# Two feed-forward layers behind a two-part attention: token blocks of 512 in three of four passes, x split chunk by chunk

## The chip, the cores and the metric

The kernel runs on one core of one Trainium2 chip. The metric is device time in microseconds of one execution; the time before is the median of three runs. A profiled execution has its own time, which stands beside its span below. TensorE (PE) has two granted clock levels, 1.2 and 2.4 GHz; the profile gives the granted clock as a share of full speed.

## The reference, cut to what matters

```python
# q, k, v: (4 batches, 8 heads, 576 positions, 64), float32
# per head: out = repeat(softmax_attention(mean4(q), mean4(k), mean4(v)), 4) + banded_attention(q, k, v, |i-j| < 4)
x = attn_out.transpose(0, 2, 1, 3).reshape(2304, 512)
h = x @ moe_w_in            # (2304, 512) @ (512, 2048)
x = silu(h) @ moe_w_out     # (2304, 2048) @ (2048, 512)
h = x @ moe2_w_in
out = elu(h) @ moe2_w_out   # (2304, 512)
```

## The kernel before

Activations lie transposed in SBUF as `x32`: 128 partitions (features within a chunk) by `KC` = 4 chunks of 128 features by 2304 tokens. Chunk c holds the heads of head pair c. A feed-forward product is made of three fp32r products (high times high, high times low, low times high), so each operand is split in a high part (`xh`, `wh`, `gh`) and a low part (`xl`, `wl`, `gl`); the high part is a cast on ACT, the low part a subtraction on DVE or POOL.

Each of the two layers runs in `NPASS` = 2 passes over the tokens, one for each half of the 16 blocks of 128 hidden features; a pass is written (layer, pass). Within a pass the loop runs over token blocks n (layer 0: nine blocks of 256; layer 1: six blocks of 384; `NBS`), and in a block over the `FP` = 8 hidden blocks f. One (layer, pass, n, f) is a unit; there are 72, 72, 48 and 48 of them. A unit has

- `g1` (line 465): 12 matmuls (4 chunks by 3 products) of the block's width into one PSUM bank `ph` (two banks in turn);
- the activation chain: in layer 0 Tanh on ACT (L476) and a DVE product (L478); in layer 1 min on DVE (L481), Exp on ACT (L482), a DVE max (L484); then the cast `gh` on ACT (L486) and the subtraction `gl` on POOL (L488);
- `g2`, emitted `LAG` = 3 units later: in layer 0 (L516) 4 output chunks by 3 matmuls of 256 columns, weights stationary, two chunks sharing a PSUM bank; in layer 1 (L518) for each 128 tokens 3 matmuls of 512 columns, `g` stationary and weights moving.

The first pass of a layer stores its sums to DRAM (`ypart`), the second loads them (`part`, one buffer) and adds: in layer 0 back into `x32`, in layer 1 into the output. After the attention is over, six PSUM banks serve the sums in turn (`ybanks`).

`split_x` makes `xh` and `xl` of the next block: one tile of 4 chunks each, two buffers, so a whole block ahead; its steps stand in the list `spread`, from which `tick` emits one step after each group of `g2` matmuls. The same list carries the decoding of weights (`decode_w`: a load into one of three `ws` buffers on SP, L154 and L156 on ACT, L165, L166 and L172 on DVE), at most 18 weight tiles ahead of their split (`split_w`, L182 and L184), which takes place in the last block of a pass.

The attention of 16 head pairs (4 batches by `NPAIR` = 4) is a generator with `STEPS` = 19 steps, several pairs under way at once. The four pairs of batch 0 run ahead of the first unit, together with the decoding of the first weights; the other twelve are fed between the matmuls of pass (0, 0) by `tick`. Pairs 0 to 3 borrow memory: their transposed rows lie in `x32` (L199), the rows of pairs 1 and 2 in the `xh` and `xl` buffers (L217), and the scores `ED` of the pooled attention go over those rows later. Later pairs have `qk` and `qkD` tiles, two buffers each. The pooled result of 144 positions is copied from PSUM to `up` (L407), and one DVE operation (L424) adds it, each position read four times, to the banded result into `x32`.

All loads are issued on SP, but for four at the very start on ACT's queue (L549). A load waits for the one that used its completion semaphore before it.

Of the kernel before, what the change touches and what calls it, by code (L numbers as in the profile page):

```python
# [22 lines left out]
def attention_moe_moe2_kernel(ctx, tc, q, k, v, wi1, wo1, wi2, wo2, out):  # L23
    nc = tc.nc
# [9 lines left out]
    NBS = (2 * P, 3 * P)  # L34
    NBM = max(NBS)
# [165 lines left out]
    def load_rows(i, which, engine=None):  # L201
        b, h0 = pairs[i][0], 2 * pairs[i][1]
        src = (q, k, v)[which]
        if which == 2:

            if i < NPAIR:
                heads = [wpool.tile([P, DM], F32R, tag=tag, name="rows2").bitcast(F32) for tag in ("wh0", "wl0")]
            else:
                t = nat.tile([P, 4 * FAC * D], F32, tag="natv", name="rows2", bufs=1)
                heads = [t[:, :DM], t[:, DM:]]  # L210
            for j, t in enumerate(heads):
                (engine or nc.sync).dma_start(t[:HS], src[b, h0 + j].rearrange("(p r) d -> p (r d)", r=2 * FAC))
# [12 lines left out]
        for j in range(2):  # L225
            (engine or nc.sync).dma_start(t[:TB, :, j * D:(j + 1) * D], src[b, h0 + j].rearrange("(c p) d -> p c d", p=TB))
        loaded[i, which] = t
# [42 lines left out]
    def attention(i):  # L270
        b, pr = pairs[i]

        if i < NPAIR:
            qk = borrow(i, "qk")
            qkD = borrow(i, "qkD")
        else:
            qk = att.tile([P, 2 * S], F32, tag="qk", name="qk")
            qkD = att.tile([P, 2 * SD], F32, tag="qkD", name="qkD")
# [3 lines left out]
        for parts in ([(0, c) for c in range(NTB - 1)], [(1, c) for c in range(NTB - 1)], [(0, NTB - 1), (1, NTB - 1)]):  # L282
            ps = bank("pst")
            for n, (which, c) in enumerate(parts):
                nc.tensor.transpose(ps[:, n * TB:(n + 1) * TB], rows[which][:TB, c, :], ident[:TB, :TB])
# [49 lines left out]

        ED = borrowed[i][:, :4 * SD] if i < NPAIR else ring("ED", 4 * SD)
        ED = ED.rearrange("p (j a s) -> p j a s", j=2, a=2)
        sm = att.tile([P, 4], F32, tag="sm", name="sm", bufs=4)

        rl2 = att.tile([P, NW, 2], F32, tag="rl2", name="rl2", bufs=4)  # L340
        nc.gpsimd.memset(rl2[:, :, 1:2], EPS)
        rl = att.tile([P, NW, 1], F32, tag="rl", name="rl", bufs=4)
# [9 lines left out]
        for j in range(2):  # L352
            ps = psd[j]
            nm = att.tile([P, 2], F32, tag="nm", name="nm", bufs=4)
            nc.vector.tensor_reduce(
                nm[:HS], ps[:HS, :2 * SD].rearrange("p (a s) -> p a s", a=2), axis=AX.X, op=ALU.max, negate=True
            )
            yield
            for a in range(2):
                nc.scalar.activation(  # L360
                    ED[:HS, j, a, :], ps[:HS, a * SD:(a + 1) * SD], AF.Exp, bias=nm[:HS, a:a + 1],
                    accum_out=sm[:HS, 2 * j + a:2 * j + a + 1],
                )
# [10 lines left out]
        ED3 = ED.rearrange("p j a s -> p (j a) s")  # L374
        nc.gpsimd.tensor_tensor(
            ED3[:HS], ED3[:HS], sm.rearrange("p (n o) -> p n o", o=1)[:HS].to_broadcast([HS, 4, SD]), ALU.mult
        )
# [13 lines left out]
        for j in range(2):  # L391
            ps = bank("psD")
            for a in range(2):
                for c in range(2):
                    o = c * SD + a * HS
                    nc.tensor.transpose(ps[:HS, o:o + HS], ED[:HS, j, a, :].rearrange("p (m c) -> p c m", c=2)[:, c, :], ident[:HS, :HS])
# [3 lines left out]
        up = att.tile([P, SD], F32, tag="up", name="up")  # L400
# [6 lines left out]
        nc.scalar.copy(up, ps[:, :SD])  # L407
        yield
        for t in range(2):
            ps = bank("pso")  # L410
            for w in range(t * NW // 2, (t + 1) * NW // 2):
# [15 lines left out]
                up[:, u0:u0 + HALF // FAC].rearrange("p (m o) -> p m o", o=1).to_broadcast([P, HALF // FAC, FAC]),  # L427
# [7 lines left out]
    def split_x(layer, ps, n):  # L435
        nb = NBS[layer]
        src = x32[:, :, n * nb:(n + 1) * nb]
        hi = xs.tile([P, KC, NBM], F32R, tag="xh", name="xh")[:, :, :nb]
        lo = xs.tile([P, KC, NBM], F32R, tag="xl", name="xl")[:, :, :nb]
        xsplit[layer, ps, n] = (hi, lo)  # L440
        for c in range(KC + 1):
            if c < KC:
                nc.scalar.copy(hi[:, c, :], src[:, c, :])
            if c > 0:
                nc.vector.tensor_tensor(lo[:, c - 1, :], src[:, c - 1, :], hi[:, c - 1, :].bitcast(F32), ALU.subtract)  # L445
            yield

# [3 lines left out]
        (layer, ps, n, f) for layer in range(2) for ps in range(NPASS) for n in range(NT // NBS[layer])  # L451
        for f in range(FP)
    ]
    g_t = {}

    def g1(u, tick):
        layer, ps, n, f = u
        nb = NBS[layer]
# [3 lines left out]
        products = [(c, a, b) for c in range(KC) for a, b in ((w[0], x[0]), (w[0], x[1]))]  # L462
        products += [(c, w[1], x[0]) for c in range(KC)]
        for k, (c, a, b) in enumerate(products):
            nc.tensor.matmul(ph[:, :nb], a[:, c, :], b[:, c, :], start=k == 0, stop=k == 3 * KC - 1)  # L465
            if k % 3 == 2:
                tick(False)
        yield
# [23 lines left out]
    def g2(u, tick):  # L492
        layer, ps, n, f = u
        nb = NBS[layer]
        g = g_t.pop(u)
        w = wt[layer, ps * FP + f, 1]
        nd = KC if layer == 0 else nb // P
        if f == 0:
            acc[0] = [ybank(f"y{d}") for d in range(KC // 2 if layer == 0 else nd)]
            if ps == 1:  # L500
                part = yp.tile([P, 4 * NBM], F32, tag="y", name="part")
                nc.sync.dma_start(part[:, :nb * KC], ypart[layer, n])
# [3 lines left out]
        if f == FP - 1 and ps == 0:  # L506
            o = yp.tile([P, 4 * NBM], F32, tag="y", name="yo")
        for d in range(nd):
            sl = slice(d * P, (d + 1) * P)
            for m in range(3):  # L510
                wm, gm = w[m // 2], g[m % 2]
                first, last = (f == 0 and m == 0), (f == FP - 1 and m == 2)
                if layer == 0:

                    h = (d % 2) * nb
                    nc.tensor.matmul(y[d // 2][:, h:h + nb], wm[:, sl], gm, start=first and d % 2 == 0, stop=last, skip_group_check=True)  # L516
                else:
                    nc.tensor.matmul(y[d], gm[:, sl], wm, start=first, stop=last)  # L518
            if f < FP - 1:
                tick(True)  # L520
                continue
            if layer == 0 and d % 2 == 0:
                continue
            i, width = (d // 2, 2 * nb) if layer == 0 else (d, DM)
            part = slice(i * width, (i + 1) * width)
            if ps == 0:
                if i % 2 == 0:
                    nc.vector.tensor_scalar_mul(o[:, part], y[i][:, :width], sc)  # L528
                else:
                    nc.scalar.activation(o[:, part], y[i][:, :width], AF.Copy, scale=sc)  # L530
            elif layer == 0:
                nc.vector.scalar_tensor_tensor(
                    x32[:, d - 1:d + 1, n * nb:(n + 1) * nb],
                    y[i][:, :width].rearrange("p (a t) -> p a t", a=2), sc,
                    acc[1][:, part].rearrange("p (a t) -> p a t", a=2), op0=ALU.mult, op1=ALU.add,
                )
            else:
                src = acc[1][:, part]
                nc.vector.scalar_tensor_tensor(src, y[i], sc, src, op0=ALU.mult, op1=ALU.add)  # L539
                t0 = n * nb + d * P  # L540
                nc.sync.dma_start(out[t0:t0 + P, :], src)
        if f == FP - 1 and ps == 0:
            ypart[layer, n] = dram.tile([P, nb * KC], F32, tag=f"yp{layer}_{n}", name=f"yp{layer}_{n}")
            nc.sync.dma_start(ypart[layer, n], o[:, :nb * KC])

    with tc.manual_schedule():
# [24 lines left out]
        def small():  # L571
            while spread:
                try:
# [3 lines left out]
                    spread.pop(0)  # L577

# [142 lines left out]
        starts = [next(n_ for n_ in range(NT // NBS[0]) if (n_ + 1) * NBS[0] > b_ * S) for b_ in range(1, B)]  # L721
        deadline = [0] + [TICKS * (FP * (n_ - 1) + 6) for n_ in starts]

        for i in range(len(units) + LAG):
            if i < len(units):
                layer, ps, n, f = units[i]
                last = NT // NBS[layer] - 1
# [11 lines left out]
                need_first(2 * f + (3 if i < FP else 0))  # L739
                at["unit"] = i  # L740
# [4 lines left out]
                if n == last and (layer, ps) != (1, 1):  # L745
# [3 lines left out]
                if f >= (6 if attending else 2):  # L749
                    nx = (layer, ps, n + 1) if n < last else ((layer, 1, 0) if ps == 0 else (layer + 1, 0, 0))  # L750
                    if nx[0] < 2 and nx not in asked:
                        asked.add(nx)
                        if nx[0] == 0 and nx[1] == 0:
                            finish(((nx[2] + 1) * NBS[0] - 1) // S)
# [4 lines left out]
            if i >= LAG:  # L759
# [4 lines left out]
                if n == NT // NBS[layer] - 1 and (layer, ps) != (1, 1):  # L764
# [31 lines left out]
```

## Time and profile before

| | |
|---|---|
| median of three runs | 989.22 us (987.25, 989.22, 989.39) |
| profiled execution, its own time | 986.26 us |
| its span, first to last instruction | 984.5 us |
| mean granted TensorE clock | 0.981 |
| pass (0, 0) begins, by its first unit | about 66 us |
| pass (0, 1), (1, 0), (1, 1) begin | 366.9, 574.2, 773.1 us |

Times in rows are microseconds from the start of the span. PE is matmuls, PEld the loads of stationary operands, which overlap them; DVE, ACT, POOL and SP are the other engines, a q behind the name is an engine's queue. Busy times of PE come from modelled ends, so the pace of PE is read here from the starts of matmuls that follow one another.

### The profile page before, as it was taken

How to read it: one execution, taken by the hardware profiler on the slowest of the kernel's cores; microseconds unless marked ns; L12 is line 12 of the kernel's file. 1: busy time of each engine (PE TensorE's matmuls, PEld its weight loads, DVE VectorE, ACT ScalarE, POOL GpSimd, SP SyncE). 2: the span in 40 equal slices, each digit the busy share in tenths (PEclk: the TensorE clock that was granted, in tenths of full speed). 3: DMA queues.
4: the chain of work that ended last, by engine and by line, in shares of the span. 5: the costliest groups of instructions: out<-in, count | busy, mean ns of one | idle time of the engine just before them, and what ended most of it. 6: DMA issues, size and time to landing. Idle time of an engine off the chain costs nothing.

```text
span 984.5 us, 18730 instructions
## 1 busy us (share of the span) xinstructions
PE 948.1 (96%) x7448; PEld 876.7 (89%) x7453; DVE 514.3 (52%) x932; ACT 449.9 (46%) x1112; POOL 366.8 (37%) x407
## 2 busy tenths in 40 slices
PE   6688999999999999999999999999999999999998
PEld 3467889999989999999999999999999999999997
DVE  5795444534538857666223366666444544424432
ACT  4684545455446675554333454444234533323221
POOL 3665453554533363232222362222223622222221
PEclk9678999999999999999999999999999999999999
DMA  9665343233114533333110002222000011101111
GB/s 210 188 175 144 77 108 92 69 97 86 39 36 129 194 107 114 123 108 108 44 38 28 23 1 86 88 84 75 1 33 33 1 65 65 65 1 65 65 46 51
DMA packets 90582, 77.74 MB, mean 79 GB/s; under 512 B 61568, under 2 KB 77952, under 8 KB 90496
## 3 DMA queue, kind: packets, MB, share of 16 engines
q1 hardware_dynamic: 88128, 75.97, 26.4%
q8 instruction: 58, 0.95, 0.4%
q10 hardware_dynamic: 2368, 0.59, 0.3%
q14 instruction: 28, 0.23, 0.1%
HBM read 62.39 MB, written 14.16 MB: 78 GB/s over the span
## 4 chain that ended last, share of the span: by engine, by line
PE 64%; DMA 1%; DVE 0%; ACT 0%; issue 0%; SPq 0%
PE ph L465 32%; PE y L518 20%; PE y L516 12%; DMA ws<-in_moe_w_in_dram 0%; DMA ws<-in_moe_w_out_dram 0%; DVE part L539 0%; ACT ws L156 0%; DVE wf L172 0%; DVE wf L166 0%; ACT t L476 0%; DVE t L478 0%; DVE wf L165 0%; ACT wf L154 0%; SPq L135 0%
## 5 line engine op out<-in xcount | busy, mean ns | idle before, releaser
L488 POOL TENSOR_TENSOR gl<-t,gh 128x256 fp32r<-128x256 f32 (+1 forms) x240 | 219.7, 915 | 517.2 <-ACT gh L486 494.7
L465 PE MATMUL ph<-xl,wh 128*128 128x256 f32 (+1 forms) x960 | 278.5, 308 | 1.6 <-DVE xl L445 1.6
L465 PE MATMUL ph<-xh,wh 128*128 128x256 f32 (+1 forms) x960 | 278.0, 308 | 1.2 <-DVE t L478 1.2
L465 PEld LDWEIGHTS ph<-xh,wh 128*128 128x128 f32 x960 | 183.5, 191 | 6.7 <-DVE t L478 1.6
L465 PEld LDWEIGHTS ph<-xl,wh 128*128 128x128 f32 x960 | 183.6, 191 | 6.4 <-DVE xl L445 2.0
L465 PE MATMUL ph<-xh,wl 128*128 128x256 f32 (+1 forms) x960 | 178.5, 306 | 0.0
L516 PE MATMUL y<-gh,wh 128*128 128x256 f32 x576 | 167.7, 291 | 1.3 <-DVE yo L528 1.3
L486 ACT CAST gh<-t 128x256 fp32r<-128x256 f32 (+1 forms) x240 | 107.8, 449 | 121.2 <-DVE t L478 71.0
L516 PE MATMUL y<-gl,wh 128*128 128x256 f32 x576 | 163.1, 283 | 0.0
L516 PE MATMUL y<-gh,wl 128*128 128x256 f32 x576 | 163.0, 283 | 0.0
L478 DVE SCALAR_TENSOR_TENSOR t<-t,ph 128x256 f32<-128x256 f32 x144 | 60.2, 418 | 182.7 <-ACT t L476 178.6
L465 PEld LDWEIGHTS ph<-xh,wl 128*128 128x128 f32 x960 | 148.9, 191 | 0.6 <-issue 0.4
L482 ACT ACTIVATE t<-t 128x384 f32<-128x384 f32 x96 | 50.5, 526 | 202.4 <-DVE t L481 202.3
L481 DVE TENSOR_SCALAR t<-ph 128x384 f32<-128x384 f32 x96 | 53.5, 557 | 134.1 <-PE ph L465 133.5
L516 PEld LDWEIGHTS y<-gh,wh 128*128 128x128 f32 x576 | 110.4, 192 | 4.5 <-issue 2.0
L518 PE MATMUL y<-wl,gh 128*128 128x512 f32 x288 | 113.9, 396 | 0.0
L518 PE MATMUL y<-wh,gl 128*128 128x512 f32 x288 | 113.7, 395 | 0.0
L518 PE MATMUL y<-wh,gh 128*128 128x512 f32 x288 | 111.9, 389 | 0.0
L476 ACT ACTIVATE t<-ph 128x256 f32<-128x256 f32 x144 | 55.1, 382 | 123.8 <-PE ph L465 121.6
L516 PEld LDWEIGHTS y<-gl,wh 128*128 128x128 f32 x576 | 110.6, 192 | 0.0
L516 PEld LDWEIGHTS y<-gh,wl 128*128 128x128 f32 x576 | 110.5, 192 | 0.0
L484 DVE SCALAR_TENSOR_TENSOR t<-t,ph 128x384 f32<-128x384 f32 x96 | 53.2, 554 | 56.8 <-ACT t L482 56.8
(90 smaller groups left out, 1213.3 us busy)
## 6 DMA issues: line engine op xcount, KB each, us to landing
ws<-in_moe_w_in_dram SPq DMA_DIRECT2D x32, 512.0 KB
ws<-in_moe_w_out_dram SPq DMA_DIRECT2D x32, 512.0 KB
rows<-in_v_dram SPq DMA_DIRECT2D x36, 144.0 KB
rows<-in_q_dram SPq DMA_DIRECT2D x32, 144.0 KB
yp<-yo SPq DMA_DIRECT2D x9, 512.0 KB
part<-yp SPq DMA_DIRECT2D x9, 512.0 KB
yp<-yo SPq DMA_DIRECT2D x6, 768.0 KB
part<-yp SPq DMA_DIRECT2D x6, 768.0 KB
```

What stands on the lines that cost most here:

```text
L465: nc.tensor.matmul(ph[:, :nb], a[:, c, :], b[:, c, :], start=k == 0, stop=k == 3 * KC - 1)
L476: nc.scalar.activation(t, h, AF.Tanh, scale=0.5)
L478: nc.vector.scalar_tensor_tensor(t, t, 1.0, h, op0=ALU.add, op1=ALU.mult)
L481: nc.vector.tensor_scalar_min(t, h, 0.0)
L482: nc.scalar.activation(t, t, AF.Exp)
L484: nc.vector.scalar_tensor_tensor(t, t, -1.0, h, op0=ALU.add, op1=ALU.max)
L486: nc.scalar.copy(gh, t)
L488: nc.gpsimd.tensor_tensor(gl, t, gh.bitcast(F32), ALU.subtract)
L516: nc.tensor.matmul(y[d // 2][:, h:h + nb], wm[:, sl], gm, start=first and d % 2 == 0, stop=last, skip_group_check=True)
L518: nc.tensor.matmul(y[d], gm[:, sl], wm, start=first, stop=last)
```

## The change

- **Blocks.** `NBS` goes. Pass (0, 0), with the attention in it, keeps nine blocks of 256 tokens. The other three passes have one block of 256 and four of 512: 40 units each. `g2` of a 512 block in layer 0 gives each output chunk a PSUM bank (`share` = 1); in layer 1 it has four groups of 128 tokens.
- **Split by chunks.** `xh` and `xl` become tiles of one chunk (128 by 512), six buffers each. Only chunks 0 and 1 of the next block are split ahead. Chunks 2 and 3 are split in `g1` of the block's last unit, whose 12 matmuls now go chunk by chunk, after the matmuls of chunk 1 and of chunk 2; they reuse the buffers of chunks 0 and 1.
- **Attention.** `qk` and `qkD` have one buffer instead of two, `rl2` two instead of four, `rl` three instead of four. The pooled result is copied, each position four times, from PSUM into `x32`, and the add works in place. The rows of pairs 1 and 2 lie in two tiles each, which takes 16 loads of 72 KB instead of 8 of 144 KB; `ED` of the first four pairs is scaled by two POOL operations instead of one.
- **Partial sums.** A 512 block of pass (0, 1) loads two stored blocks of 256 into one tile.

```diff
+    WIDE = [(0, 2 * P)] + [(t_, 4 * P) for t_ in range(2 * P, NT, 4 * P)]
+    BLOCKS = {(0, 0): [(t_, 2 * P) for t_ in range(0, NT, 2 * P)], (0, 1): WIDE, (1, 0): WIDE, (1, 1): WIDE}
...
-            t = xs.tile([P, KC * NBM], F32R, tag=("xh", "xl")[which], name=f"rows{which}").bitcast(F32)
-            borrowed[2 * i - 2 + which] = t
+            ts = [xs.tile([P, NBM], F32R, tag=("xh", "xl")[which], name=f"rows{which}", bufs=6).bitcast(F32) for _ in range(2)]
+            half = NTB // 2
+            for j in range(2):
+                for a in range(2):
+                    (engine or nc.sync).dma_start(
+                        ts[a][:TB, :half * 2 * D].rearrange("p (c e) -> p c e", c=half)[:, :, j * D:(j + 1) * D],
+                        src[b, h0 + j].rearrange("(c p) d -> p c d", p=TB)[:, a * half:(a + 1) * half],
+                    )
+                borrowed[2 * i - 2 + which, j] = ts[j]
...
-            qk = att.tile([P, 2 * S], F32, tag="qk", name="qk")
-            qkD = att.tile([P, 2 * SD], F32, tag="qkD", name="qkD")
+            qk = att.tile([P, 2 * S], F32, tag="qk", name="qk", bufs=1)
+            qkD = att.tile([P, 2 * SD], F32, tag="qkD", name="qkD", bufs=1)
...
-        up = att.tile([P, SD], F32, tag="up", name="up")
+        up = x32[:, pr, b * S:(b + 1) * S].rearrange("p (m r) -> p m r", r=FAC)
...
-        nc.scalar.copy(up, ps[:, :SD])
+        nc.scalar.copy(up, ps[:, :SD].rearrange("p (m o) -> p m o", o=1).to_broadcast([P, SD, FAC]))
...
+    def split_x(layer, ps, n, first=0):
+
+        t0, nb = BLOCKS[layer, ps][n]
+        src = x32[:, :, t0:t0 + nb]
+        hi, lo = xsplit.setdefault((layer, ps, n), ([], []))
+        last = first + 1 if first else KC if (layer, ps, n) == (0, 0, 0) else 2
+        for c in range(first, last + 1):
+            if c < last:
+                hi.append(xs.tile([P, NBM], F32R, tag="xh", name="xh", bufs=6)[:, :nb])
+                nc.scalar.copy(hi[c], src[:, c, :])
+            if c > first:
+                lo.append(xs.tile([P, NBM], F32R, tag="xl", name="xl", bufs=6)[:, :nb])
+                nc.vector.tensor_tensor(lo[c - 1], src[:, c - 1, :], hi[c - 1].bitcast(F32), ALU.subtract)
             yield
...
+        if f == FP - 1:
+
+            products = [(c, w[m // 2], x[m % 2]) for c in range(KC) for m in range(3)]
+        else:
+            products = [(c, w[0], x[m]) for c in range(KC) for m in range(2)]
+            products += [(c, w[1], x[0]) for c in range(KC)]
+        for m, (c, a, b) in enumerate(products):
+            nc.tensor.matmul(ph[:, :nb], a[:, c, :], b[c], start=m == 0, stop=m == 3 * KC - 1)
+            if m % 3 == 2:
                 tick(False)
+                if f == FP - 1 and c in (1, 2) and following(u):
+                    nx = following(u)
+                    while len(xsplit.get(nx, ((), ()))[1]) < c + 1:
+                        small_step[0]()
+                    for _ in split_x(*nx, c + 1):
+                        pass
...
+        share = 2 if layer == 0 and nb == 2 * P else 1
...
-                    h = (d % 2) * nb
-                    nc.tensor.matmul(y[d // 2][:, h:h + nb], wm[:, sl], gm, start=first and d % 2 == 0, stop=last, skip_group_check=True)
+                    h = (d % share) * nb
+                    nc.tensor.matmul(y[d // share][:, h:h + nb], wm[:, sl], gm, start=first and d % share == 0, stop=last, skip_group_check=True)
...
-                tick(True)
+                for _ in range(KC // nd):
+                    tick(True)
```

## Rows read from the trace of the kernel before

**Rows 1.** The page: busy time by engine, and the clock in 40 slices
```profile
PE 948.1 (96%) x7448; PEld 876.7 (89%) x7453; DVE 514.3 (52%) x932; ACT 449.9 (46%) x1112; POOL 366.8 (37%) x407
PEclk9678999999999999999999999999999999999999
```

**Rows 2.** Windows by stage: stretch, length, busy us of each engine, clock, DMA, GB/s
```profile
0.00:66.14 66.14, 47.31 (x524) 30.22 (x529) 47.76 (x93) 42.82 (x115) 38.85 (x54) 0.79 0.85 192
66.14:294.00 227.86, 214.95 (x2548) 198.74 (x2545) 112.17 (x236) 113.95 (x363) 109.84 (x137) 0.98 0.33 87
366.86:574.22 207.36, 207.36 (x1730) 207.36 (x1729) 100.70 (x185) 95.00 (x230) 69.59 (x80) 1.00 0.22 70
773.14:972.02 198.88, 198.88 (x1000) 180.40 (x999) 80.93 (x137) 62.14 (x124) 53.98 (x51) 1.00 0.13 48
```

**Rows 3.** Timeline of PE in pass (0, 1): first g1 matmul of two successive units
```profile
499.34 0.28 PE L465 MATMUL ph<-xh,wh 128*128 128x256 f32 x1
...
502.22 0.28 PE L465 MATMUL ph<-xh,wh 128*128 128x256 f32 x1
```

**Rows 4.** Chain that ended last: into layer 1, then 84 unit starts
```profile
574.39 2.08 PE ph L465 x12
577.90 2.08 PE ph L465 x12
...
622.59 2.10 PE ph L465 x12
...
970.08 2.10 PE ph L465 x12
```

**Rows 5.** Timeline of PE in layer 1: one unit, then the last g2 units
```profile
622.42 0.33 PE L465 MATMUL ph<-xh,wh 128*128 128x384 f32 x1
...
624.53 0.39 PE L518 MATMUL y<-wh,gh 128*128 128x512 f32 x1
...
626.61 0.33 PE L465 MATMUL ph<-xh,wh 128*128 128x384 f32 x1
...
974.10 0.39 PE L518 MATMUL y<-wh,gh 128*128 128x512 f32 x1
...
980.00 0.39 PE L518 MATMUL y<-wl,gh 128*128 128x512 f32 x1
```

**Rows 6.** Groups by shape: busy us, mean ns | idle before
```profile
L182 ACT CAST wh<-wf 128x512 fp32r<-128x512 f32 x64 | 38.3, 613 | 1.6 <-DVE wf L172 1.5
L445 DVE TENSOR_TENSOR xl<-x,xh 128x256 fp32r<-128x256 f32 x72 | 38.9, 562 | 9.8 <-ACT xh L443 9.7
L184 DVE TENSOR_TENSOR wl<-wf,wh 128x512 fp32r<-128x512 f32 x24 | 23.4, 982 | 6.8 <-ACT wh L182 6.2
L443 ACT CAST xh<-x 128x256 fp32r<-128x256 f32 x72 | 25.8, 402 | 0.8 <-DVE x L424 0.8
L407 ACT COPY up<-psu 128x144 f32<-128x144 f32 x16 | 4.5, 280 | 2.4 <-PE psu L404 2.3
L293 ACT ACTIVATE qk<-pst 128x480 f32<-128x480 f32 x12 | 6.7, 560 | 3.6 <-PE pst L285 3.6
L329 POOL TENSOR_TENSOR vt<-rows 72x256 f32<-72x256 f32 x32 | 22.7, 729 | 6.4 <-DMA rows<-in_v_dram 6.2 <-POOL E L322 0.2
L375 POOL TENSOR_TENSOR rows<-rows,sm 72x576 f32<-72x576 f32 x4 | 4.6, 1144 | 0.0
```

**Rows 7.** The DMA queues in the first 30 us, 40 slices of busy tenths
```profile
DMA  0039999999999999999999999999999989989998
```

**Rows 8.** Timeline of SP and ACT at the start: loads, and a wait
```profile
0.73 3.96 SPq L226 DMA_DIRECT2D rows<-in_q_dram  x6
21.03 0.62 ACT L154 ACTIVATE pw<-ws 128x512 f32<-128x512 f32 x1 [3.67 <-DMA ws<-in_moe_w_out_dram]
```

**Rows 9.** PE's waits before the first unit: total us, times, longest
```profile
PE psD L396 <- ACT rows L360: 5.8, 2, 4.3
PE psl L307 <- ACT x L295: 5.8, 3, 5.1
```

More of the change, by code (lines that the diff above doesn't have):

```diff
@@ L216, in load_rows @@
         if i in (1, 2):
-            t = xs.tile([P, KC * NBM], F32R, tag=("xh", "xl")[which], name=f"rows{which}").bitcast(F32)
-            borrowed[2 * i - 2 + which] = t
+            ts = [xs.tile([P, NBM], F32R, tag=("xh", "xl")[which], name=f"rows{which}", bufs=6).bitcast(F32) for _ in range(2)]
[7 more added lines that the diff above has]
+                borrowed[2 * i - 2 + which, j] = ts[j]
+            loaded[i, which] = [t[:, c * 2 * D:(c + 1) * 2 * D] for t in ts for c in range(half)]
+            return
         elif i == 3 and which == 0:
@@ L226, in load_rows @@
             (engine or nc.sync).dma_start(t[:TB, :, j * D:(j + 1) * D], src[b, h0 + j].rearrange("(c p) d -> p c d", p=TB))
-        loaded[i, which] = t
+        loaded[i, which] = [t[:, c] for c in range(NTB)]
     def load_windows(i):
@@ L284, in attention @@
             for n, (which, c) in enumerate(parts):
-                nc.tensor.transpose(ps[:, n * TB:(n + 1) * TB], rows[which][:TB, c, :], ident[:TB, :TB])
+                nc.tensor.transpose(ps[:, n * TB:(n + 1) * TB], rows[which][c][:TB], ident[:TB, :TB])
             o = 0
@@ L334, in attention @@
             load_windows(i)
[L336 to L337 removed]
+        if i < NPAIR:
+            ED = [borrowed[i, j][:, :2 * SD].rearrange("p (a s) -> p a s", a=2) for j in range(2)]
+            EDs = [(x, slice(2 * j, 2 * j + 2)) for j, x in enumerate(ED)]
+        else:
+            ED = ring("ED", 4 * SD).rearrange("p (n s) -> p n s", n=4)
+            EDs = [(ED, slice(0, 4))]
+            ED = [ED[:, 0:2], ED[:, 2:4]]
         sm = att.tile([P, 4], F32, tag="sm", name="sm", bufs=4)
[L340 removed]
+        rl2 = att.tile([P, NW, 2], F32, tag="rl2", name="rl2", bufs=2)
         nc.gpsimd.memset(rl2[:, :, 1:2], EPS)
[L342 removed]
+        rl = att.tile([P, NW, 1], F32, tag="rl", name="rl", bufs=3)
         psd = [bank("psd"), bank("psd")]
@@ L360, in attention @@
                 nc.scalar.activation(
-                    ED[:HS, j, a, :], ps[:HS, a * SD:(a + 1) * SD], AF.Exp, bias=nm[:HS, a:a + 1],
+                    ED[j][:HS, a, :], ps[:HS, a * SD:(a + 1) * SD], AF.Exp, bias=nm[:HS, a:a + 1],
                     accum_out=sm[:HS, 2 * j + a:2 * j + a + 1],
@@ L373, in attention @@
         nc.vector.reciprocal(sm[:HS], sm[:HS])
[L374 to L377, printed above, removed]
+        for x, heads in EDs:
+            n = heads.stop - heads.start
+            nc.gpsimd.tensor_tensor(
+                x[:HS], x[:HS], sm[:, heads].rearrange("p (n o) -> p n o", o=1)[:HS].to_broadcast([HS, n, SD]), ALU.mult
+            )
         yield
@@ L433, in attention_moe_moe2_kernel, with following, last_block @@
     xsplit = {}
[L435 to L445, printed above, removed]
-            yield
+    def split_x(layer, ps, n, first=0):
[10 more added lines that the diff above has]
+                nc.vector.tensor_tensor(lo[c - 1], src[:, c - 1, :], hi[c - 1].bitcast(F32), ALU.subtract)
+            yield
+    def following(u):
+        layer, ps, n, _ = u
+        if n + 1 < len(BLOCKS[layer, ps]):
+            return layer, ps, n + 1
+        if ps + 1 < NPASS:
+            return layer, ps + 1, 0
+        return (layer + 1, 0, 0) if layer == 0 else None
     ypart = {}
     units = [
-        (layer, ps, n, f) for layer in range(2) for ps in range(NPASS) for n in range(NT // NBS[layer])
-        for f in range(FP)
+        (layer, ps, n, f) for layer in range(2) for ps in range(NPASS)
+        for n in range(len(BLOCKS[layer, ps])) for f in range(FP)
     ]
     g_t = {}
+    small_step = []
+    def last_block(u):
+        return u[2] == len(BLOCKS[u[0], u[1]]) - 1
     def g1(u, tick):
         layer, ps, n, f = u
-        nb = NBS[layer]
+        nb = BLOCKS[layer, ps][n][1]
         ph = ps_h.tile([P, 512], F32, tag="h", name="ph")
@@ L461, in g1 @@
         w = wt[layer, ps * FP + f, 0]
[L462 to L466, printed above, removed]
-                tick(False)
+        if f == FP - 1:
+            products = [(c, w[m // 2], x[m % 2]) for c in range(KC) for m in range(3)]
+        else:
+            products = [(c, w[0], x[m]) for c in range(KC) for m in range(2)]
[3 more added lines that the diff above has]
+            if m % 3 == 2:
+                tick(False)
+                if f == FP - 1 and c in (1, 2) and following(u):
[4 more added lines that the diff above has]
+                        pass
         yield
@@ L493, in g2 @@
         layer, ps, n, f = u
-        nb = NBS[layer]
+        t0, nb = BLOCKS[layer, ps][n]
         g = g_t.pop(u)
@@ L497, in g2 @@
         nd = KC if layer == 0 else nb // P
+        share = 2 if layer == 0 and nb == 2 * P else 1
         if f == 0:
-            acc[0] = [ybank(f"y{d}") for d in range(KC // 2 if layer == 0 else nd)]
+            acc[0] = [ybank(f"y{d}") for d in range(nd // share)]
             if ps == 1:
                 part = yp.tile([P, 4 * NBM], F32, tag="y", name="part")
-                nc.sync.dma_start(part[:, :nb * KC], ypart[layer, n])
+                for t1, width, kept in ypart[layer]:
+                    if t0 <= t1 < t0 + nb:
+                        if layer == 0:
+                            dst = part[:, :KC * nb].rearrange("p (d t) -> p d t", d=KC)[:, :, t1 - t0:t1 - t0 + width]
+                            nc.sync.dma_start(dst, kept.rearrange("p (d t) -> p d t", d=KC))
+                        else:
+                            nc.sync.dma_start(part[:, :nb * KC], kept)
                 acc[1] = part
@@ L720, in attention_moe_moe2_kernel @@
         clock = [0]
-        starts = [next(n_ for n_ in range(NT // NBS[0]) if (n_ + 1) * NBS[0] > b_ * S) for b_ in range(1, B)]
+        starts = [next(n_ for n_ in range(NT // NB0) if (n_ + 1) * NB0 > b_ * S) for b_ in range(1, B)]
         deadline = [0] + [TICKS * (FP * (n_ - 1) + 6) for n_ in starts]
@@ L739, in attention_moe_moe2_kernel @@
                 need_first(2 * f + (3 if i < FP else 0))
+                while len(xsplit[layer, ps, n][1]) < KC:
+                    small()
                 at["unit"] = i
@@ L744, in attention_moe_moe2_kernel @@
                 tail.append(rest)
-                if n == last and (layer, ps) != (1, 1):
+                if last_block(units[i]) and (layer, ps) != (1, 1):
                     split(nc.gpsimd)
@@ L749, in attention_moe_moe2_kernel @@
                 if f >= (6 if attending else 2):
-                    nx = (layer, ps, n + 1) if n < last else ((layer, 1, 0) if ps == 0 else (layer + 1, 0, 0))
-                    if nx[0] < 2 and nx not in asked:
+                    nx = following(units[i])
+                    if nx and nx not in asked:
                         asked.add(nx)
-                        if nx[0] == 0 and nx[1] == 0:
-                            finish(((nx[2] + 1) * NBS[0] - 1) // S)
+                        if nx[:2] == (0, 0):
+                            finish(((nx[2] + 1) * NB0 - 1) // S)
                         spread.insert(0, split_x(*nx))
@@ L763, in attention_moe_moe2_kernel @@
                 layer, ps, n, f = u
-                if n == NT // NBS[layer] - 1 and (layer, ps) != (1, 1):
+                if last_block(u) and (layer, ps) != (1, 1):
                     split(nc.vector)
```

37 lines of the change are left out of this document (18 added, 19 removed).

## The prediction

> **What bounds the kernel now.** I read the page first. PE is busy 96% of the span and no other engine more than 52%, and the granted clock is full (2.4 GHz) from about the fifth of the 40 slices on [rows 1]. A busy PE is not yet a PE at its peak, so I went on to the windows by stage. The span falls in two parts. Up to 66 us PE works 47 of 66 us, DVE 48 and ACT 43, and in pass (0, 0) up to 294 us PE works 215 of 228. There the other engines and the attention have a say. From 366.9 us on PE is busy for the whole length of each window (207.36 of 207.36 us in pass (0, 1), 198.88 of 198.88 in pass (1, 1)), while DVE, ACT and POOL are busy at most half of it [rows 2]. The last 620 us are therefore set by how fast PE takes one matmul after another, and the chain that ended last runs there from unit to unit through matmuls alone [rows 4]. So I need the pace, from start to start.
>
> In pass (0, 1) a unit takes 502.22 - 499.34 = 2.88 us for 24 matmuls of 256 columns, 0.120 us each [rows 3]. 256 columns at 2.4 GHz are 0.1067 us: 13.3 ns of each matmul are no columns. At the end, where only `g2` is left, 26 steps of 512 columns take 980.00 - 974.10 = 5.90 us, 0.2269 us each [rows 5]: 512 columns are 0.2133 us, and again 13.6 ns are left. So a matmul costs its columns and a fixed 13.5 ns or so, and what counts is the number of matmuls.
>
> Layer 1 has a little more. Its unit takes (970.08 - 622.59) / 83 = 4.187 us [rows 4]. 12 matmuls of 384 columns (0.160 + 0.0133 = 0.1733 us) and 9 of 512 (0.2269) make 4.122, so 0.065 us a unit is over. In the unit at 622.42 the 384-column matmuls take 2.11 / 12 = 0.176 us and the 512-column ones 2.08 / 9 = 0.231 [rows 5]: both kinds are slower there. On the way from layer 0 to layer 1, where 12 matmuls of 384 columns stand beside 12 of 256, the step is 577.90 - 574.39 = 3.51 us against 12 x 0.1733 + 12 x 0.120 = 3.52 [rows 4]: nothing is over. The extra goes with the `g2` of layer 1 (`g` stationary, 512 columns), not with wide matmuls in `g1`.
>
> **The change: fewer, wider matmuls.** Pass (0, 1) goes from 72 x 24 = 1728 matmuls to 40 x 24 = 960. Before it took 72 x 2.88 = 207.4 us. After, the block of 256 takes 8 x 2.88 = 23.0 us and the four of 512 take 32 x 24 x 0.2269 = 174.3, together 197.3: 10.1 us saved. If a 512-column matmul costs 0.231 as in the mixed unit, they take 177.4, and 6.9 us are saved.
>
> A pass of layer 1 keeps its `g2` matmuls (18 groups of 128 tokens) and goes from 48 x 12 to 40 x 12 in `g1`. Before: 48 x 4.187 = 201.0 us. After, if each unit keeps its 0.065 us: 8 x (12 x 0.120 + 6 x 0.2269 + 0.065) = 22.9, and 32 x (24 x 0.2269 + 0.065) = 176.3, together 199.2: 1.8 us a pass, 3.5 for both. If every 512-column matmul costs 0.231 it is 0.9 a pass, 1.8 for both; if the extra goes away with the mixture of widths, 196.7 and 8.6 for both. I keep the extra, as the rows have it wherever this `g2` meets a `g1`. Both terms: 13.6 us, between 8.7 and 18.7.
>
> The Trainium skill ("TensorE: Matmul & The Clock Gate", section "Back-to-back issue gap") gives the gap of a warm matmul as its columns at 2.4 GHz and about 2.5 ns. By that the 768 + 192 = 960 matmuls that go would save 960 x 2.5 ns = 2.4 us, and with the costs below nothing would be left. The trace disagrees with it: 13.3 ns at 256 columns here.
>
> **What could stop PE in these passes.** The chunks: chunks 2 and 3 of the next block are now split only while the last unit's `g1` runs, since they reuse the buffers of chunks 0 and 1. For 512 columns, chunk 0 is free after 3 matmuls (0.68 us), chunk 1 after 6 (1.36 us). The cast takes about as long as that of a 512-column weight, 0.61 us, the subtraction on DVE 0.98 [rows 6]: chunk 3 is ready at some 1.36 + 0.61 + 0.98 = 3.0 us, a little more with signals. It is wanted by the seventh matmul of the next `g1`, after 12 + 12 + 6 matmuls or 6.8 us. Some 3.5 us are left for what stands ahead in the ACT and DVE queues. The casts wait on ACT for PE's third and sixth matmul; behind them stands the Tanh or Exp of the same unit, which waits for all 12 anyway. I put this at nothing; without the cover it would be a few tenths at each of 12 borders.
>
> PSUM: a 512 block takes four of six banks, so the next one starts in the two free ones and comes to a used one 1.4 us into its own first `g2`, after the old bank was emptied during the last `g2` and a whole `g1` of 2.7 us. Partial sums: the load of 1 MB has seven units, 38 us. Weights: 16 tiles must be decoded per pass; a decode is asked for at every second unit outside the last block, so 32 units give 16, just enough, and each unit is longer. `g2` comes three units behind `g1`, 16 us, for a chain of five operations. All this at nothing.
>
> **The attention.** The copy of the pooled result grows from 144 to 576 columns: 0.28 us at 144, 0.56 at 480 on the same engine [rows 6], so 0.64, 0.36 more. Twelve of them lie in pass (0, 0), where ACT is busy half the time; four, 1.4 us, before the first unit. Scaling `ED` there takes two POOL operations of 288 columns instead of one of 576: between 0.73 at 256 and 1.14 at 576 that is 0.77 each, 0.4 more for each of four pairs, 1.6 in all. The single `qk` buffer: a pair starts when the one before has done six steps, and by then its score matmuls stand ahead of the new transposes in PE's own order. Nothing.
>
> The loads of rows for pairs 1 and 2 become 16 instead of 8, six more on SP and two more on ACT. The first six of SP took 3.96 us, 0.66 each [rows 8], so SP could come up to 4 us later to the first weights and v rows; and ACT stands still up to 3.7 us for such weights [rows 8], with PE behind it [rows 9]. Against it, the queues are full from 2 to 30 us [rows 7] and carry the same bytes: what is issued later waits less. I take half of ACT's 1.4 us and POOL's 1.6, nothing for the loads: +1.5 us, between -1 (the first split no longer waits for two pairs' rows) and +5.
>
> The borders of pass (0, 0): nine blocks, eight borders inside. Chunk 0 is free 0.36 us into the last `g1`, and chunk 2 is wanted 0.12 x (12 + 12 + 4) = 3.4 us into it; cast and subtraction take 0.40 + 0.56 [rows 6]. Two microseconds are left for queues that carry attention work. Often enough; I take 1 us for all, between 0 and 6.
>
> **Sum.** -13.6 + 1.5 + 1 = -11 us. The profiled execution took 986.26 us for a span of 984.5, so 975.2; it lies 3.0 us below the median of the three runs (989.22), and from there it is 978.2. I say 977.
>
> **Rivals.** (1) The borders lose more than the width gains: ACT, which takes work in order, holds the attention's copies behind a cast that waits for PE, and PE then waits for those copies. For: PE waited on ACT in the busy start [rows 9]. Against: in pass (0, 0) ACT is busy 114 of 228 us [rows 2]. It decides from (13.6 - 1.5) / 8 = 1.5 us a border; at 2.5 us the time is 989 - 12 + 20 = 997. Chance 7%. (2) Wide matmuls in `g1` are no cheaper by the column: 0.240 us at 512. Then pass (0, 1) gains nothing, layer 1 takes 32 x (12 x 0.240 + 12 x 0.231) + 22.6 = 203.5 a pass, 5 more for both, and the time is about 996. Against it are the 26 steps of 0.2269. 3%. (3) The start slips by the SP queue, up to 5 us: 981. 7%, still faster. (4) The extra 0.065 us is a matter of mixed widths and goes: 972. 15%. (5) Weights come late in a pass with half the units, or only the few nanoseconds of the page count: what is won is lost again, 987 to 990. 6%. My forecast, 970 to 983, has 62%.
>
> Range: 967 to 986, with the high gain and no costs at one end, the low gain and 5 us of costs at the other. Faster by over 0.2% (about what a measurement can tell from no change) 86%, within it 6%, slower 8%.
>
> **What would show it.** Right: starts 0.227 us apart in `g1` and `g2` of pass (0, 1), units of 5.45 us there and about 5.5 in layer 1, (0, 1) about 197 us long, no waits of PE after it, first unit at 66 to 69 us, pass (0, 1) starting at 367 to 371. Wrong: PE waiting at borders for `xl` or `xh`, starts near 0.24 us apart, or a pass (0, 1) that begins 10 us later.

## The result and the profile after

The changed kernel takes 978.73 us in the median of six runs, against 989.31 for the kernel before, a ratio of 0.9894 with a 95% interval of 0.9851 to 0.9936. It was timed twice more beside other kernels: 0.9859 (0.9818 to 0.9901) and 0.9875 (0.9846 to 0.9904). Over all timed runs of this study the mean is 978.2 us for 18 runs of the changed kernel and 990.4 for 51 of the kernel before (its four sets have means of 990.1 to 990.9): 12.2 us less. The profiled execution took 978.92 us with a span of 977.1.

The page of the changed kernel (busy us, share of span, instructions; clock in 40 slices):

```profile
PE 935.5 (96%) x6493; PEld 805.0 (82%) x6493; DVE 511.7 (52%) x841; ACT 439.4 (45%) x995; POOL 353.1 (36%) x363
PEclk9677999999999999999999999999999999999999
```

PE takes about a thousand instructions fewer than in [rows 1] and is still the busy engine. Where the time went is seen in windows cut at the first `g1` matmul of each pass, and in pass (0, 0) also after 48 of its 72 units, at 302.09 us (columns as in [rows 2]):

```profile
0.00:72.11 72.11, 48.97 (x530) 31.31 (x530) 48.60 (x93) 44.35 (x116) 39.84 (x58) 0.76 0.81 178
72.11:302.09 229.98, 218.95 (x2572) 202.41 (x2569) 112.33 (x241) 119.63 (x368) 110.11 (x137) 0.97 0.33 86
302.09:376.16 74.07, 71.74 (x579) 70.90 (x577) 52.44 (x92) 48.28 (x107) 30.00 (x30) 0.98 0.47 143
376.16:569.53 193.37, 193.37 (x963) 164.75 (x961) 99.00 (x133) 82.97 (x152) 61.13 (x49) 1.00 0.23 71
569.53:768.34 198.81, 197.47 (x914) 164.41 (x912) 117.65 (x163) 83.22 (x150) 60.18 (x48) 1.00 0.15 51
768.34:973.30 204.96, 204.96 (x949) 171.21 (x947) 80.98 (x122) 60.92 (x106) 51.87 (x43) 1.00 0.13 48
```

Pass (0, 1) lasts 193.4 us instead of 207.4 [rows 2]. Of the 14.0 us, 3.8 are only moved: three `g2` of 512 columns lie beyond the cut and three of 256 came in from the pass before, 3 x (2.72 - 1.44). Pass (1, 0) is no shorter than before by these cuts (198.8 against 198.9 us). Its first three units of before have `g2` of 256 columns from layer 0 and take about 2 us less than its others, 3 x (4.187 - 3.51) by [rows 4], so that like for like some 2 us are saved; and PE idles in it for 1.3 us. From the start of pass (0, 1) to the end it is 977.1 - 376.16 = 600.9 us, where it was 984.5 - 366.9 = 617.6: 16.7 us won. Ahead of it, 9.3 us are lost, 6.0 of them before the first unit (72.1 instead of 66.1 us), so that the two profiled executions differ by 7.3 us.

The pace is in two views. The chain that ended last, in the middle of pass (0, 1) and of pass (1, 0):

```profile
482.65 2.72 PE ph L501 x12
485.37 2.72 PE y L565 x12
488.09 2.72 PE ph L501 x12
...
643.38 2.72 PE ph L501 x12
646.10 2.72 PE y L567 x12
648.82 2.72 PE ph L501 x12
```

A unit of 512 columns takes 5.44 us in either layer, 0.2267 us a matmul. The 0.065 us that a unit of layer 1 had over its matmuls [rows 4] are gone.

PE's waits from the last 24 units of pass (0, 0) on (us in total, times, longest):

```profile
PE ph L501 <- ACT xh L462: 2.2, 2, 1.6
PE ph L501 <- DVE t L526: 0.9, 1, 0.9
PE ph L501 <- DVE xl L465: 0.4, 1, 0.4
```

The first are at two borders of pass (0, 0), near 325 and 352 us, where PE waits for the high part of a late chunk; the other two lie at the end of the block of 256 of pass (1, 0), near 596 and 598 us. ACT's timeline says why the chunk is late at 325 us (in brackets the idle time before, and what ended it):

```profile
322.85 0.67 ACT L157 ACTIVATE wf<-ws 128x512 f32<-128x512 f32 x1 [2.59 <-DMA ws<-in_moe_w_out_dram]
323.41 0.67 ACT L159 ACTIVATE ws<-ws 128x512 uint32<-128x512 uint32 x1
323.98 0.37 ACT L518 ACTIVATE t<-ph 128x256 f32<-128x256 f32 x1
324.84 0.41 ACT L528 CAST gh<-t 128x256 fp32r<-128x256 f32 x1 [0.49 <-DVE t L520]
325.80 0.67 ACT L157 ACTIVATE wf<-ws 128x512 f32<-128x512 f32 x1 [0.56 <-DMA ws<-in_moe_w_in_dram]
326.37 0.69 ACT L159 ACTIVATE ws<-ws 128x512 uint32<-128x512 uint32 x1
326.96 0.68 ACT L462 CAST xh<-x 128x256 fp32r<-128x256 f32 x2
```

ACT stands still 2.6 and again 0.6 us for weights that have not landed, and the two casts (L462) that PE needs next come behind them in its order. Before the change ACT waits for weights in these 24 units too (5.5 us in all, the longest 1.5, against 8.5 and 2.6 here), but PE has no wait for `xh`: the block had been split a block ahead.

### The profile page after: what moved, and what is told of

Same layout as the page of the kernel before. It is cut to its first block, busy times and chain, and to the rows that moved or that the text cites. A ratio compares the mean times of both kernels' runs of the same rounds, so it can differ in the third digit from the quotient of the medians.

```text
span 977.1 us, 16442 instructions
## 1 busy us (share of the span) xinstructions
PE 935.5 (96%) x6493; PEld 805.0 (82%) x6493; DVE 511.7 (52%) x841; ACT 439.4 (45%) x995; POOL 353.1 (36%) x363
## 4 chain that ended last, share of the span: by engine, by line
PE 62%; ACT 1%; DVE 1%; issue 1%; DMA 0%; SPq 0%; DVEq 0%; ACTq 0%
PE ph L501 31%; PE y L567 19%; PE y L565 12%; DMA ws<-in_moe_w_out_dram 0%; DVE part L588 0%; DVE t L523 0%; ACT t L524 0%; ACT xh L462 0%; DVE xl L465 0%; ACT ws L159 0%; ACT gh L528 0%; ACT wf L157 0%; ACT wh L185 0%; DVE wf L169 0%; DVE wf L168 0%
## 5 line engine op out<-in xcount | busy, mean ns | idle before, releaser
L501 PEld LDWEIGHTS ph<-xh,wh 128*128 128x128 f32 x768 | 146.5, 191 | 21.6 <-ACT xh L462 2.8
L501 PEld LDWEIGHTS ph<-xl,wh 128*128 128x128 f32 x768 | 146.5, 191 | 19.1 <-DVE xl L465 3.2
L565 PE MATMUL y<-gh,wh 128*128 128x256 f32 (+1 forms) x448 | 146.1, 326 | 1.3 <-DVE yo L578 1.3
L565 PE MATMUL y<-gl,wh 128*128 128x256 f32 (+1 forms) x448 | 141.2, 315 | 0.0
L565 PE MATMUL y<-gh,wl 128*128 128x256 f32 (+1 forms) x448 | 141.1, 315 | 0.0
L520 DVE SCALAR_TENSOR_TENSOR t<-t,ph 128x256 f32<-128x256 f32 (+1 forms) x112 | 55.3, 494 | 160.3 <-ACT t L518 159.4
L524 ACT ACTIVATE t<-t 128x512 f32<-128x512 f32 (+1 forms) x80 | 47.1, 589 | 195.6 <-DVE t L523 195.6
L523 DVE TENSOR_SCALAR t<-ph 128x512 f32<-128x512 f32 (+1 forms) x80 | 51.0, 637 | 122.3 <-PE ph L501 121.9
L518 ACT ACTIVATE t<-ph 128x256 f32<-128x256 f32 (+1 forms) x112 | 49.6, 443 | 116.4 <-PE ph L501 113.8
L465 DVE TENSOR_TENSOR xl<-x,xh 128x256 fp32r<-128x256 f32 (+1 forms) x96 | 69.4, 740 | 45.1 <-ACT xh L462 43.4
```

Source lines behind the costliest of these rows:

```text
L465: nc.vector.tensor_tensor(lo[c - 1], src[:, c - 1, :], hi[c - 1].bitcast(F32), ALU.subtract)
L501: nc.tensor.matmul(ph[:, :nb], a[:, c, :], b[c], start=m == 0, stop=m == 3 * KC - 1)
L518: nc.scalar.activation(t, h, AF.Tanh, scale=0.5)
L520: nc.vector.scalar_tensor_tensor(t, t, 1.0, h, op0=ALU.add, op1=ALU.mult)
L523: nc.vector.tensor_scalar_min(t, h, 0.0)
L524: nc.scalar.activation(t, t, AF.Exp)
```

## The experiments

The runs are numbered first to eleventh, in the order in which their expectations stand here. Ratios are against the kernel before, timed beside each set. In the pieces of code, `...` stands for lines left out.

**Half loads alone.** The kernel before, with only the 16 smaller loads:

```diff
...
+            half = NTB // 2
+            for j in range(2):
+                for a in range(2):
+                    (engine or nc.sync).dma_start(
+                        t[:TB, a * half:(a + 1) * half, j * D:(j + 1) * D],
+                        src[b, h0 + j].rearrange("(c p) d -> p c d", p=TB)[:, a * half:(a + 1) * half],
+                    )
...
```

> The kernel before, with one part of the change alone: the rows of pairs 1 and 2 come in 16 loads of 72 KB instead of 8 of 144 KB, into the same tiles. Theory (eight loads may be under way at a time, so smaller ones leave the DMA engines short of work and the first weights land later): first weight work on ACT at 18 to 20 us instead of 15.7, first unit at 70 to 72 us instead of 66.1, time 4 to 6 us above before. Rival (the start is late because of the longer copy of the pooled result and the two POOL operations, and the loads are hidden): first unit at 66 to 67 us, time as before.

It took 990.71 us, a ratio of 0.9994 (0.9972 to 1.0015; 12 runs). The theory falls. In the profile its signs are there: the first weight work on ACT at 17.9 us, the first unit at 72.9 us, and the DMA queues of the first 30 us (40 slices) have the gap that [rows 7] have not:

```profile
DMA  0029999999866669997899999987999999989999
```

But the time says that at most 1.5 us come of it (the upper end of the interval). The profiled execution (994.40 us) is the slowest of this kernel's runs, and that of the kernel before (986.26) one of the fastest of its own. So the first units of single profiles, which I had taken for the theory's proof, are no proof: two later profiles with the same instructions up to there begin theirs at 68.9 and 73.1 us (sixth and ninth run).

**The old widths.** The changed kernel with blocks of 256 and 384 columns:

```diff
+    W256 = [(t_, 2 * P) for t_ in range(0, NT, 2 * P)]
+    W384 = [(t_, 3 * P) for t_ in range(0, NT, 3 * P)]
+    BLOCKS = {(0, 0): W256, (0, 1): W256, (1, 0): W384, (1, 1): W384}
```

> The changed kernel with the block widths of before (256 in layer 0, 384 in layer 1), all else as changed. Theory (all that is won comes from the widths, and the extra 0.065 us of a layer 1 unit comes from neighbouring matmuls of 384 and 512 columns): units of 2.88 and 4.187 us, time 16 to 19 us above the changed kernel, that is 994 to 998, slower than before. Rival (the extra goes because x now lies in tiles of one chunk, or for another reason than the widths): units of 4.12 us in layer 1, time 988 to 991.

994.47 us (10 runs), 1.0044 (1.0021 to 1.0066) of the kernel before: all that is not width makes the kernel slower, by 994.4 - 990.4 = 4 us in the means. From pass (0, 1) on its profile is that of the kernel before, so these 4 us lie ahead of it. The widths then win 994.4 - 978.2 = 16.2 us. Its windows of passes (0, 1) and (1, 0), and its chain in layer 1:

```profile
375.67:583.03 207.36, 207.36 (x1731) 207.36 (x1729) 101.60 (x184) 96.03 (x229) 70.47 (x80) 1.00 0.22 70
583.03:781.96 198.93, 198.93 (x1019) 181.35 (x1018) 118.23 (x183) 85.91 (x168) 61.59 (x56) 1.00 0.14 50
```

```profile
602.10 2.10 PE ph L503 x12
...
618.85 2.10 PE ph L503 x12
```

To the hundredth the passes of before [rows 2], and the step of 16.75 / 4 = 4.188 us is back: the extra belongs to units that mix 384 and 512 columns, not to the way in which x is stored.

**Two chunks of a 256 block in a tile.** The changed kernel, with every block of 256, and every block after one, split whole ahead again:

```diff
-        last = first + 1 if first else KC if (layer, ps, n) == (0, 0, 0) else 2
+        last = first + 1 if first else KC if nb == 2 * P or xs_free(layer, ps, n) else 2
+        per = NBM // nb
...
+                if c % per == 0:
+                    th[0] = xs.tile([P, NBM], F32R, tag="xh", name="xh", bufs=6)
+                hi.append(th[0][:, c % per * nb:(c % per + 1) * nb])
...
```

> The changed kernel, but blocks of 256 tokens put two chunks in one tile of 512 columns, so that a block that follows a block of 256, and each block of 256, is split whole ahead as before the change. Theory (PE's waits at 325, 352 and 596 us come from the last two chunks being split late, behind ACT's waits for weights): these waits go but for the one of 0.7 us that the kernel before has too; pass (0, 0) 300 to 301 us long instead of 304.1, and 1 to 2 us less in pass (1, 0); start as in the changed kernel, 72 us; time 972 to 975. Rival (the waits come from weights that land late, whatever the order of the splits): PE waits as long for weights or for the chain, time 977 to 979.

979.21 us, 0.9873 (0.9842 to 0.9903). In the trace the theory holds for pass (0, 0): PE's waits for `xh` there are gone, and the last 24 units of the pass, the stretch with both waits, take

```profile
307.53:377.79 70.26, 69.62 (x578) 69.22 (x577) 53.12 (x93) 48.07 (x108) 30.04 (x30) 1.00 0.48 151
```

70.3 us instead of 74.1. In the kernel before they take 69.9:

```profile
296.96:366.86 69.90, 69.37 (x578) 69.17 (x577) 53.28 (x93) 48.06 (x108) 30.86 (x30) 1.00 0.47 152
```

The theory fails for pass (1, 0), which stays at 198.8 us: the wait for `xl` went and another grew, 1.5 us for the chain on DVE. And the time does not fall with it: in this profile the first unit begins at 76.5 us, against 72.1, and what pass (0, 0) wins is gone before it starts. Whether the one has to do with the other, this run does not show.

**Tiles of 1024 columns in three buffers.** The third experiment with whole loads and one POOL operation:

```diff
-            ts = [xs.tile([P, NBM], F32R, tag=("xh", "xl")[which], name=f"rows{which}", bufs=6).bitcast(F32) for _ in range(2)]
+            t = xs.tile([P, 2 * NBM], F32R, tag=("xh", "xl")[which], name=f"rows{which}", bufs=3).bitcast(F32)
...
-                    th[0] = xs.tile([P, NBM], F32R, tag="xh", name="xh", bufs=6)
+                    th[0] = xs.tile([P, 2 * NBM], F32R, tag="xh", name="xh", bufs=3)
...
```

> The third experiment with tiles of 1024 columns in three buffers instead of 512 in six (four chunks of a 256 block, two of a 512 block in one), so that the rows of pairs 1 and 2 fit one tile and come in 8 loads of 144 KB as before, and ED of the first four pairs is scaled by one POOL operation. Theory (loads): first unit at 66 to 68 us, time 966 to 970. Rival (the start is late because of the copy of the pooled result): first unit at 70 to 72 us, time 972 to 975.

973.63 us, 0.9830 (0.9794 to 0.9866), first unit at 69.2 us: the start lies between the two and the time is the rival's, so it was run again beside the changed kernel and with the loads and the POOL operation put back one by one.

> The changed kernel once more, beside the next three on one chip, since the part before pass (0, 1) differs by some microseconds from run to run. From pass (0, 1) on the same stages as in its first profile, 193.4, 198.8 and 208.7 us, to a tenth; time 977 to 981.

975.94 us, the three late stages 193.4, 198.8 and 208.7 us as expected, the first unit at 71.4.

> The fourth experiment once more (tiles of 1024 columns, loads of 144 KB, one POOL operation for ED). If its gain of about 5 us on the changed kernel is real, 971 to 975, with pass (0, 1) beginning at 367 to 372 us; if it was the luck of the run, 977 to 981.

975.80 us, 0.9837 (0.9803 to 0.9871); pass (0, 1) begins at 367.8 us. Over twelve runs this version's mean is 974.4 us; the changed kernel's is 978.2 over eighteen. Some 4 us are real, with an uncertainty of about 1.3 (the standard error of the difference).

The seventh run has the edit of the first experiment, in these tiles; the eighth this one:

```diff
-        EDs = [(ED, slice(0, 4))]
+        EDs = [(ED[:, 0:2], slice(0, 2)), (ED[:, 2:4], slice(2, 4))] if i < NPAIR else [(ED, slice(0, 4))]
```

> The fourth experiment with the rows of pairs 1 and 2 loaded in halves of 72 KB again, into the same tiles. Theory (the smaller loads cost the start most of what the changed kernel loses before its first unit): 3 to 5 us above the sixth run. Rival (the first experiment's time is right, and smaller loads cost about 1 us): 0 to 2 us above it.

> The fourth experiment with ED of the first four pairs scaled by two POOL operations of 288 columns instead of one of 576, all else as there. Theory (loads): 0 to 1 us above the sixth run. Rival (POOL's extra operations, 1.6 us together, and what waits behind them are what the start loses): 3 to 5 us above it.

972.96 and 977.22 us, 0.9841 (0.9798 to 0.9883) and 0.9840 (0.9804 to 0.9877), beside 0.9837 for the sixth run. Neither the loads nor the POOL operations, each by itself, cost anything that these runs can tell; but six runs beside twelve have a standard error of about 2 us, so a cost of 3 or 4 us is not excluded here, and for the loads it is the first experiment, in the kernel before, that excludes it. By the trace some 3 of the 4 us would lie at the borders (the last 24 units of pass (0, 0) take 71.1 us in the sixth run, and 74.1, 72.6 and 73.5 in the changed kernel's three profiles). The third experiment speaks against that: it has the same gain there, and is no faster in the mean of all its runs (978.2 us over twelve, with the tenth run). Loads and POOL operations together, and the larger tiles by themselves, were not tried. So where the 4 us come from is not shown.

**Decoding in the wide blocks.**

```diff
-                elif not attending and (i % 2 or (layer, ps) == (0, 0)):
+                elif not attending and ((layer, ps) == (0, 0) or BLOCKS[layer, ps][n][1] == NBM):
```

> The fourth experiment, but in passes (0, 1) and (1, 0) a decode of a weight is asked for at every unit of a 512 block and none in the block of 256, instead of at every second unit. Theory (PE's wait in the block of 256 of pass (1, 0) comes from decode operations that stand ahead of the chain on DVE, with a unit of 2.8 us too short for both): that wait, 1.5 us, goes, and the pass takes about 196.5 us by its matmuls instead of 198.5; time 2 us below the sixth run. Rival (the chain itself is too long for such short units, or the splits are late): the wait stays.

971.71 us, 0.9817 (0.9775 to 0.9858). PE has no wait left after pass (0, 0), and pass (1, 0), by windows of the sixth run and of this one:

```profile
561.16:759.64 198.48, 197.00 (x913) 164.58 (x912) 116.98 (x164) 83.10 (x151) 59.65 (x48) 1.00 0.15 51
```

```profile
567.81:764.45 196.64, 196.64 (x914) 164.65 (x912) 112.77 (x161) 82.73 (x151) 60.04 (x48) 1.00 0.15 49
```

takes 1.8 us less, as expected: the decode operations had stood ahead of the chain. This is the fastest version of the study by its median. The time alone would not tell it from the sixth run (intervals overlap); the trace does.

> The third experiment once more, beside the changed kernel. By its trace it saves about 3 us in pass (0, 0); its first times showed nothing. If the borders are worth what the trace says, 2 to 4 us below the next run; else equal.

> The changed kernel for the third time, for the comparison with the run before: 975 to 980, waits of PE near 325 and 352 us as in its first profile, unless they are a matter of the run.

979.67 us for the third experiment again, 976.69 for the changed kernel. The changed kernel has its waits near 325 and 350 us in all three profiles; its last 24 units of pass (0, 0) take 74.1, 72.6 and 73.5 us. The third experiment has neither wait in either of its profiles (70.3 and 70.2 us) and begins its first unit late in both (76.5 and 75.4 us). Whether its packing makes the start late or both were unlucky is open: the start differs by 4 us between kernels that are alike up to there. The sixth and the ninth run issue the same instructions up to pass (0, 1), and yet, in windows of 0 to 40, 40 to 80 and 140 to 165 us, first the sixth, then the ninth:

```profile
0.00:40.00 40.00, 25.75 (x274) 15.05 (x274) 24.10 (x50) 20.81 (x58) 20.40 (x37) 0.83 0.96 193
40.00:80.00 40.00, 31.22 (x311) 23.13 (x312) 33.41 (x61) 31.29 (x75) 24.28 (x24) 0.77 0.67 178
140.00:165.00 25.00, 23.65 (x281) 21.76 (x281) 12.64 (x27) 12.78 (x42) 13.32 (x18) 1.00 0.25 60
```

```profile
0.00:40.00 40.00, 25.76 (x274) 14.78 (x274) 24.68 (x51) 21.47 (x60) 21.14 (x37) 0.83 0.93 194
40.00:80.00 40.00, 33.50 (x296) 24.35 (x296) 30.67 (x56) 28.61 (x69) 21.63 (x21) 0.66 0.60 156
140.00:165.00 25.00, 23.64 (x296) 21.13 (x295) 13.80 (x28) 10.87 (x36) 11.12 (x13) 0.86 0.32 74
```

PE has the same work behind it at 40 us, but the granted clock (the column after the five busy times) is 0.66 instead of 0.77 in the next 40, and 0.86 instead of 1.00 later. Pass (0, 1) begins at 374.4 instead of 367.8 us. The same split goes through other profiles: the first, third, eighth and tenth run have 0.59 to 0.67 and 0.86 in these two windows and begin their first unit at 72.9 to 76.5 us; the kernel before, the fourth and the seventh run have 0.75 to 0.79 and 1.00 and begin it at 66.1 to 70.6; the changed kernel's three and the second run lie between (0.74, 0.86 to 1.00, 71.1 to 72.1 us). Whether the lower clock makes the start late, or a PE that waits longer lowers the clock, no run here separates. A single profile of this kernel says nothing of the first 370 us to better than some 7 us.

## Why the prediction was right

The forecast was 977 us from a median of 989.2, so 12 less; the mean of all runs is 12.2 less. That it fits so well is partly two errors that cancel.

**The pace and pass (0, 1): right.** Units of 24 x 0.2267 = 5.44 us. With the 3.8 us that only move, the 40 units take 197.2 us against the forecast 197.3, and 10.1 us are saved. The fixed 13.3 ns of each matmul at 256 columns are there at 512 as well, and the mechanism, fewer matmuls, carries the result. The rival of 0.240 us at 512 is out. The Trainium skill ("TensorE: Matmul & The Clock Gate", section "Back-to-back issue gap") gives 2.5 ns beside the columns, for a matmul by itself; by that the saving would be an estimated 2.4 us. The trace has 13.3 ns, and the widths won 16.2 us.

**Layer 1: fewer matmuls right, the extra misread, the term too small.** I put the extra 0.065 us of a unit down to the `g2` of layer 1, kept it "as the rows have it wherever this `g2` meets a `g1`", and gave the case that it is a matter of mixed widths 15%. It is that: units of 5.44 us in layer 1, and 4.188 again with the old widths. The term of 3.5 us was 8.6 for the matmuls alone.

**What could stop PE: wrong at one place.** "All this at nothing" held for PSUM, the partial sums, the borders between wide blocks and the end. It did not hold at the block of 256 of pass (1, 0), which takes 198.8 us where 196.6 are enough (ninth run). Most of it is the weights: units of 2.8 us are too short for the chain and a decode every second unit, and 1.8 us go when no decode is asked for there (sixth against ninth run). Some 0.3 us more go with the split ahead (198.8 in the changed kernel, 198.5 in the sixth run), where PE had waited for `xl`. So the late passes win 10.1 + 8.6 - 2.2 = 16.5 us, where I had 13.6; the traces have 16.7 and the times 16.2.

**The attention part: too small.** I had 1.5 us for the start and 1 for the borders; together they are 4, by the second experiment. How they divide is not settled. By the traces the borders are most of it, though the times of the third experiment do not bear it out: the last 24 units of pass (0, 0) take 2.7 to 4.2 us more than before in the three profiles, all at two borders. I had the mechanism (two microseconds left for queues in order) and its bound of 6, but looked for it among the attention's work, and the first borders cost nothing that shows (the first 48 units take 230.0 us, and 230.8 before, from 66.14 to 296.96). It came where ACT waits for weights, late in the pass. Rival (1) needed 1.5 us at each of eight borders and is out. The loads at nothing was right to 1.5 us (first run), and the POOL operations, put at half of 1.6 us, do not show (eighth run, which could not have seen less than some 4 us). What is left for the start, about 1 us, is within what these runs can't tell.

**Signs.** Those of the pace came, but not all of the others. The first unit began at 72.1, 71.4 and 71.6 us in the three profiles, where I had said 66 to 69; pass (0, 1) has 193.4 us between its cuts, since I had left out the 3.8 that only move; PE waits twice after it, for 0.9 and 0.4 us; and one sign of being wrong, PE waiting at borders for `xh`, did appear, with 1.9 to 2.8 us in all. That the time still fits is in part luck. Pass (0, 1) began at 376.2, 373.9 and 375.0 us, where I had said 367 to 371. Most of that is in the reference: the profile of before that I counted from was a fast one, some 4 us below its kernel's mean, and its luck lay all in the part before pass (0, 1): from there on it takes 617.6 us, and the first experiment's profile, of the same work there and 8 us slower, 617.1.

## What to carry to other kernels

Where PE is busy from one matmul to the next, read the time from start to start at two widths; what is left over the columns is the price of a matmul. Where a unit's matmuls all have one width, before and after, the number saved gave the gain to a few per cent here (pass (0, 1), 10.1 us); where widths mix, as in layer 1, look for a further price of the mixture. When buffers are cut so that work must happen just in time, look at what stands ahead of it in its engine's order, a wait for a DMA above all. And where two single profiles differ in a part that varies from run to run, time the suspect alone before believing in it.

## What the runs showed of the hardware

A change to 512 columns costs a little, at the first matmuls after it. At the end of pass (0, 1)'s first block, where a `g1` of 512 columns follows a `g2` of 256 (timeline of PE of the changed kernel):

```profile
399.20 0.40 PE L501 MATMUL ph<-xh,wh 128*128 128x512 f32 x1
...
400.36 0.39 PE L501 MATMUL ph<-xl,wh 128*128 128x512 f32 x1
400.59 0.39 PE L501 MATMUL ph<-xh,wh 128*128 128x512 f32 x1
400.81 0.39 PE L501 MATMUL ph<-xl,wh 128*128 128x512 f32 x1
```

The first five steps take 1.16 / 5 = 0.232 us each, then the pace is back at 0.227. In units of 384 and 512 columns both sides pay, 0.065 us a unit; in units of one width nothing is paid, and between 384 and 256 columns nothing shows [rows 4]. What in the chip does it, no run here shows.

A wait of PE can cost more than itself. In the profile of the changed kernel the stretch with the two border waits has a granted clock of 0.98 over 74 us: PE waited at 325 us, and soon after the clock was at its lower level (1.2 GHz, half of full speed) for some 3 us:

```profile
327.80:331.20 3.40, 3.35 (x15) 3.35 (x16) 3.24 (x7) 2.50 (x6) 1.14 (x1) 0.51 0.50 154
```

PE is busy 71.7 us in these 24 units there, and 70.6 in the two other profiles of this kernel, which have the waits and a granted clock of 1.00 throughout.
